# Rounding the weights in two stages: the first piece in two halves, and the first unit's scores ahead of the last sums

## The chip, the cores and the metric

The kernel runs on one core of one Trainium2 chip. The time of a run is the device time of that core in microseconds (us), and the metric is the median of several runs. A core has a matrix engine (PE, TensorE), three engines for element-wise work (DVE or VectorE, ACT or ScalarE, POOL or GpSimd), a queue that starts transfers (SP, SyncE) and 16 engines that carry them out. Each engine works through its own list of instructions in order and waits for the others by semaphores.

## The reference

Attention that keeps the 32 largest scores of every row, followed by a two-layer network with a leaky ReLU. There are 8 batches of 8 heads, with 576 positions and 64 values per head; the network has 4608 tokens, 512 inputs and 2048 hidden values.

```python
scores = scale * np.matmul(q, k.transpose(0, 1, 3, 2))
kth = np.partition(scores, -top_k, axis=-1)[..., -top_k:-top_k + 1]
scores = np.where(scores >= kth, scores, -1000000000.0)
attn = np.exp(scores - np.max(scores, axis=-1, keepdims=True))
attn = attn / (np.sum(attn, axis=-1, keepdims=True) + 1e-09)
x = np.matmul(attn, v)        # heads side by side: (4608, 512)
h = x @ w_in                  # (4608, 2048)
out = np.maximum(0.01 * h, h) @ w_out
```

The inputs q, k and v are 32-bit floats. The two weight matrices are 64-bit floats, and have to be turned into 32-bit floats by the kernel.

## The kernel before

**Rounding the weights (lines 84 to 150 and 492 to 511).** Both weight matrices together are cut into 16 pieces of 128 partitions by 1024 columns. Each 64-bit number is loaded as four 16-bit words, so a piece is 1 MB. `load_weights(n)` starts the load of piece n into one of three `raw` buffers. `round_weights(n)` is a generator with three stages:

- Stage 1: POOL copies the top word of each number into a 16-bit tile `top` (L124). ACT turns the third word into a float (L125), and the lower two words into a bf16 (L127).
- Stage 2: DVE takes the exponent out of `top` (L129, into the tile `scale`), the top bits of the mantissa (L132, into a tile that has the name `wT`), and the sign (L133, in place). ACT raises 2 to the exponent (L131). PE adds up the three parts of the mantissa: for each half of 512 columns three products with scaled identity matrices (L143, L144, L145), which the text calls the sums.
- Stage 3: DVE joins sign and power of two (L147) and multiplies the sums by it (L150).

The loop of lines 495 to 500 issues, in iteration n, stage 1 of piece n, stage 2 of piece n-1 and stage 3 of piece n-2. The order in which these calls are made is the order of the instructions on each engine. Then follows the load of piece n+3. The tiles `top` and `scale` have two buffers each, so POOL's copy for piece n waits until L147 of piece n-2 has read `top`. A load of piece n+3 waits until L124, L125 and L127 of piece n have read the raw buffer. PSUM holds the sums in the tiles `wide` (two buffers, pieces 0 to 11), `narrow` (one, pieces 12 and 14) and `ml` (two, pieces 13 and 15).

**The first scores.** In the iterations n = 12 to 15 the loads of q and k for the first four head pairs are started (`load_qk`), and the loads of v in n = 15. In iteration 14 `first_scores` issues the products of unit 0 (L231) on PE and the two copies of its scores from PSUM on ACT (L236); in iteration 16 it does so for unit 1.

**The rest.** A unit is 128 rows of queries of two heads. The main loop runs one step per unit: DVE finds the 32 largest scores (`top_k`, lines 238 to 255, which begins with L245), POOL masks, ACT takes exponents, the weights are transposed by transfers through DRAM, PE weighs the values, and PE works off the network for finished tokens in between, by budgets in the code. The order is written out by hand, nothing is reordered.

Of the kernel before, what the change touches and what calls it, by code (L numbers as in the profile page):

```python
# [20 lines left out]
def kernel(  # L21
# [78 lines left out]
    def load_weights(n):  # L100
        if n >= NPIECE:
            return
        if not AS_WORDS:
            nc.sync.dma_start(piece(n), weights[n])
            return
        raw_of[n] = raws.tile([P, WCH, 4], U16, name="raw")
        nc.sync.dma_start(raw_of[n].rearrange("p n w -> p (n w)"), weights[n])

    def round_weights(n):

        raw = raw_of.pop(n)
        dst = piece(n)
        mid = raw[:, :, 2]
        low = raw.rearrange("p n w -> p (n w)").bitcast(U32).rearrange("p (n w) -> p n w", w=2)[:, :, 0]
        top = raws.tile([P, WCH], U16, name="top", bufs=2)
        scale = raws.tile([P, WCH], U16, name="scale", bufs=2)  # L120
        parts = work.tile([P, 2 * NKC - 1, P], F32, name="wT", bufs=3)
        parts = parts.rearrange("p c n -> p (c n)").bitcast(U16)
        m_top, m_low = parts[:, 0:WCH], parts[:, WCH:2 * WCH].bitcast(BF16)
        nc.gpsimd.tensor_copy(top, raw[:, :, 3])  # L124
        nc.scalar.activation(dst, mid, AF.Copy, bias=-7.0 - 2.0 ** -16, scale=2.0 ** -20)  # L125

        nc.scalar.activation(m_low, low, AF.Copy, bias=128.0, scale=2.0 ** -29)  # L127
        yield
        nc.vector.tensor_scalar(scale, top, 4, 0x7FF, ALU.logical_shift_right, ALU.bitwise_and)  # L129

        nc.scalar.activation(scale.bitcast(BF16), scale, AF.Exp, bias=least, scale=LN2)  # L131
        nc.vector.tensor_scalar(m_top, top, 0xF, 0x3F80, ALU.bitwise_and, ALU.bitwise_or)  # L132
        nc.vector.tensor_scalar(top, top, 0x8000, None, ALU.bitwise_and)  # L133
        if n < NPIECE - 4 or n % 2 == 0:
            tag, bufs = ("wide", 2) if n < NPIECE - 4 else ("narrow", 1)
            pw = ps_sc.tile([P, 2, 512], F32, name=tag, bufs=bufs)
            sums = [(pw[:, h, :], h * 512) for h in range(2)]
            ends = [(pw.rearrange("p h n -> p (h n)"), 0)]
        else:
            ends = sums = [(ps_ml.tile([P, 512], F32, name="pw", tag="ml"), h * 512) for h in range(2)]  # L140
        for pw, c in sums:
            at = slice(c, c + 512)
            nc.tensor.matmul(pw, ident_top, m_top[:, at].bitcast(BF16), start=True, stop=False)  # L143
            nc.tensor.matmul(pw, ident, dst[:, at], start=False, stop=False)  # L144
            nc.tensor.matmul(pw, ident_low, m_low[:, at], start=False, stop=True)  # L145
        yield
        nc.vector.tensor_tensor(scale, scale, top, ALU.bitwise_or)  # L147
        for pw, c in ends:
            at = slice(c, c + pw.shape[-1])
            nc.vector.tensor_tensor(dst[:, at], pw, scale[:, at].bitcast(BF16), ALU.mult)  # L150
# [73 lines left out]
    def first_scores(u):  # L224

        ps = [ps_sc.tile([P, 2, 512], F32, name="wide", bufs=2) for i in range(2)]
        for half in range(2):
            for i, pi, side, r0 in u.parts:
                qt, kt = qk_of[pi]
                d = slice(side * D, (side + 1) * D)  # L230
                nc.tensor.matmul(ps[i][:, half, 0:HS], qt[d, u.q0:u.q0 + P],  # L231
                                 kt[d, half * HS:(half + 1) * HS], start=True, stop=True)
        u.both = work.tile([P, 2, S], F32, name="s_sb", bufs=5)
        u.s = [u.both[:, i, :] for i in range(2)]
        for i in range(2):
            nc.scalar.copy(u.s[i].rearrange("p (h n) -> p h n", h=2), ps[i][:, :, 0:HS])  # L236
# [243 lines left out]
    with tc.manual_schedule():  # L480
        last = {p: n for n, u in enumerate(steps) for p in u.pairs}

        def load_more(s):

            for of, load, n, lag in ((v_of, load_v, LOADED_V, LAG + 1), (qk_of, load_qk, LOADED + 3, 8)):
                while len(of) < NPAIR and (len(of) < n or last[len(of) - n] + lag <= s):
                    load(len(of))
                    if lag > LAG + 1 and len(of) > n:
                        break


        for n in range(3):
            load_weights(n)
        rounding = {}
        for n in range(NPIECE + 2):
            for i in (n, n - 1, n - 2) if AS_WORDS else ():
                if 0 <= i < NPIECE:
                    if i == n:
                        rounding[i] = round_weights(i)
                    next(rounding[i], None)  # L500
            load_weights(n + 3)

            if NPIECE - HP <= n < NPIECE:
                load_qk(n - NPIECE + HP)
            if n == NPIECE - 2:
                first_scores(steps[0])
            elif n == NPIECE:
                first_scores(steps[1])
            if n == NPIECE - 1:
                load_v(0)  # L510
                load_v(1)

        def weights_of(u):
            reciprocals(u)
            normalize(u, 0)
            normalize(u, 1)

        def values(*place):
            due = [u for n, u in enumerate(steps) if values_at(n) == place]
            if due:  # L520
                po = ps_sc.tile([P, 2, 512], F32, name="wide", bufs=2)[:, 0, 0:2 * P]
# [126 lines left out]
```

## Time and profile before

| | |
|---|---|
| median of 3 runs | 1468.14 us (1467.84 to 1468.83) |
| span of the profiled execution, first to last instruction | 1467.8 us |
| mean granted TensorE clock | 0.982 |
| busy, whole span | PE 1393.7 us (95%), DVE 1319.9 (90%), ACT 1099.8 (75%), POOL 1096.2 (75%) |
| busy, 0 to 63.54 us | PE 49.74 us, DVE 48.82, ACT 54.08, POOL 18.76; transfer engines 93% |
| moved by transfers | 222.29 MB, mean 151 GB/s; 342 GB/s from 0 to 63.54 us |

The span is the profiled execution's own time as the page gives it; the runs' median stands 0.3 us above it. At 63.54 us the first instruction of `top_k` starts on DVE, and the rounding of the weights is over. In the lines shown below, "L150 DVE ..." is line 150 of the kernel and the engine that runs it; an entry such as `w_in<-wide,scale` names the tile that is written and those that are read; "x2" says that a row joins two instructions; and a bracket gives how long the engine had been idle before, and the engine, tile and line that released it. The rows of digits cut the span in 40 slices and give the busy share of each in tenths.

### The profile page before, as it was taken

Reading aid. Unit: us, or ns where it says so; the run is one execution under the profiler, and the core shown is the slowest. Engines: PE = TensorE matmul, PEld = TensorE weight load, DVE = VectorE, ACT = ScalarE, POOL = GpSimd, SP = SyncE. Lnnn points to the kernel's source line nnn. Section 1 sums busy time; section 2 is a strip of 40 time slices with the busy share of each in tenths; the row PEclk is TensorE's granted clock in tenths of the full one; section 3 lists DMA queues with packets and bytes.
Section 4 is the critical chain, followed back from the end, with each engine's and each line's share of the span. In section 5 each row is a group of like instructions: output and inputs, shape, how many; then the busy total and the mean of one; then the engine's idle time right before and its main releaser. Section 6 shows DMA issues by size and latency. Waiting matters only on the chain.

```text
span 1467.8 us, 24094 instructions
## 1 busy us (share of the span) xinstructions
PE 1393.7 (95%) x8068; PEld 927.3 (63%) x8068; DVE 1319.9 (90%) x3396; ACT 1099.8 (75%) x1981; POOL 1096.2 (75%) x743
## 2 busy tenths in 40 slices
PE   7716999999999999999999999999999999999999
PEld 2304548575757676767676767666666666666674
DVE  6999999999999999999999999999999999999600
ACT  8657888777887777777777777777777777777710
POOL 3288888888788888787878888878787878787700
PEclk9957999999999999999999999999999999999999
DMA  9824443654376455664566544766566545664510
GB/s 332 299 81 130 138 119 112 174 153 137 101 194 192 129 137 155 171 185 137 146 170 190 141 137 129 191 178 150 127 168 200 140 135 138 161 138 136 146 46 14
DMA packets 388795, 222.29 MB, mean 151 GB/s; under 512 B 333888, under 2 KB 333888, under 8 KB 386624
## 3 DMA queue, kind: packets, MB, share of 16 engines
q1 hardware_dynamic: 388672, 220.77, 53.9%
q8 instruction: 63, 1.03, 0.3%
q14 instruction: 60, 0.49, 0.1%
HBM read 46.14 MB, written 92.01 MB: 94 GB/s over the span
## 4 chain that ended last, share of the span: by engine, by line
PE 85%; DVE 10%; ACT 2%; DMA 2%; issue 1%; POOL 0%; DVEq 0%; SPq 0%; ACTq 0%
PE ph L386 32%; PE pz L398 31%; PE wide L330 11%; PE wide L215 6%; DVE tops L250 3%; PE narrow L215 3%; DVE pairs L253 3%; DMA wT<-apart 1%; PE ph L354 1%; DVE pairs L245 1%; DVE w_in L150 1%; ACT split L288 1%; DVE scale L147 1%; ACT s_sb L222 1%; DVE w_out L150 1%
## 5 line engine op out<-in xcount | busy, mean ns | idle before, releaser
L263 POOL TENSOR_SCALAR pen<-s_sb,tops 128x576 f32<-128x576 f32 x288 | 637.5, 2214 | 209.2 <-DVE tops L250 139.0
L250 DVE MAX8 tops<-pairs 128x8 f32<-128x288 f32 (+1 forms) x1152 | 635.9, 591 | 0.0
L398 PE MATMUL pz<-w_out,gT 128*128 128x512 f32 x1152 | 504.7, 594 | 2.4 <-ACT scale L359 2.4
L386 PE MATMUL ph<-x,w_in 128*128 128x256 f32 x2176 | 482.7, 381 | 0.0
L253 DVE MATCH_REPLACE8 pairs<-tops,pairs 128x288 f32<-128x288 f32 (+1 forms) x864 | 460.1, 538 | 0.0
L386 PEld LDWEIGHTS ph<-x,w_in 128*128 128x128 f32 x2176 | 409.4, 190 | 76.5 <-issue 22.2
L264 POOL TENSOR_TENSOR s_sb<-s_sb,pen 128x576 f32<-128x576 f32 x288 | 406.5, 1412 | 24.1
L398 PEld LDWEIGHTS pz<-w_out,gT 128*128 128x128 f32 x1152 | 216.4, 190 | 267.2 <-issue 262.8
L288 ACT COPY split<-s_sb 128x1152 uint16<-128x1152 uint16 x280 | 309.4, 1146 | 0.0
L279 ACT ACTIVATE s_sb<-s_sb,rz 128x576 f32<-128x576 f32 x288 | 207.6, 772 | 45.5 <-DVE rz L276 45.5
L267 ACT ACTIVATE s_sb<-s_sb,nbias 128x576 f32<-128x576 f32 x288 | 222.2, 772 | 15.2 <-POOL s_sb L264 15.2
L245 DVE TENSOR_TENSOR pairs<-s_sb 128x576 f32<-128x576 f32 x288 | 213.4, 780 | 10.3 <-ACT s_sb L279 0.5
L330 PEld LDWEIGHTS wide<-wT,vt 128*64 128x64 f32 x3200 | 161.2, 139 | 68.0 <-issue 35.0
L330 PE MATMUL wide<-wT,vt 128*64 128x128 f32 (+1 forms) x3200 | 179.0, 268 | 25.5 <-ACT s_sb L222 22.1
L222 ACT COPY s_sb<-wide 128x704 f32<-128x704 f32 x142 | 107.1, 755 | 21.4 <-PE wide L215 21.4
L392 ACT ACTIVATE gT<-ph 128x512 f32<-128x512 f32 x136 | 80.6, 592 | 54.2 <-PE ph L386 53.5
L344 ACT COPY x<-wide 128x128 f32<-128x128 f32 (+1 forms) x160 | 32.2, 260 | 112.9 <-PE wide L330 112.8
L215 PE MATMUL wide<-kt,qt 64*128 64x352 f32 (+1 forms) x392 | 74.6, 490 | 28.8 <-ACT s_sb L222 24.9
L407 ACT COPY o_sb<-pz 128x512 f32<-128x512 f32 x36 | 21.1, 585 | 97.5 <-PE pz L398 97.5
L222 ACT COPY s_sb<-narrow 128x448 f32<-128x448 f32 x142 | 68.7, 536 | 0.7
L276 DVE RECIPROCAL rz<-ze 128x2 f32<-128x2 f32 x144 | 22.2, 154 | 45.7 <-ACT ze L272 45.5
L253 DVE MATCH_VALUE_LOAD pairs<-tops,pairs 128x8 f32 x864 | 62.5, 72 | 0.0
(61 smaller groups left out, 623.2 us busy)
## 6 DMA issues: line engine op xcount, KB each, us to landing
apart<-split SPq DMA_DIRECT2D x280, 288.0 KB, 2.1
raw<-in_weights_dram SPq DMA_DIRECT2D x16, 1024.0 KB, 5.8
vt<-in_vk_dram SPq DMA_DIRECT2D x32, 320.0 KB, 3.8
out_dram<-o_sb SPq DMA_DIRECT2D x36, 256.0 KB, 2.6
qt<-in_qT_dram SPq DMA_DIRECT2D x20, 288.0 KB, 3.5
kt<-in_kT_dram SPq DMA_DIRECT2D x20, 288.0 KB, 3.7
raw<-in_qT_dram SPq DMA_DIRECT2D x12, 288.0 KB, 3.5
raw<-in_kT_dram SPq DMA_DIRECT2D x12, 288.0 KB, 3.8
```

What stands on the lines that cost most here:

```text
L215: nc.tensor.matmul(to[r0:r0 + u.rows, i, :], qt[d, u.q0:u.q0 + u.rows], kt[d, k0:k1], start=True, stop=True)
L245: nc.vector.tensor_tensor(pairs[:, :, n, :], u.both[:, :, 0:HS], u.both[:, :, HS:S], op)
L250: nc.vector.max(out=u.tops[:, i, r, :], in_=rest[i])
L253: nc.vector.match_replace(out=rest[i], in_to_replace=u.tops[:, i, r, :], in_values=rest[i], imm_value=LOWEST)
L263: nc.gpsimd.tensor_scalar(pen, u.s[i], u.tops[:, i, ROUNDS - 1, 7:8], MASKED, ALU.is_lt, ALU.mult)
L264: nc.gpsimd.tensor_tensor(u.s[i], u.s[i], pen, ALU.add)
L267: nc.scalar.activation(u.s[i], u.s[i], AF.Exp, bias=u.nbias[:, i:i + 1], scale=SCALE, accum_out=u.z[:, i:i + 1])
L279: nc.scalar.activation(u.s[i], u.s[i], AF.Copy, bias=0.0, scale=u.rz[:, i:i + 1])
L288: nc.scalar.copy(split, pairs[:, :, h])
L330: nc.tensor.matmul(po[side * D:(side + 1) * D, o, :], vt[:, c, side, :], u.wT[:, c + side * NKC if c + 1 < NKC else c, r:r + n], start=(c ...
L386: nc.tensor.matmul(ph[:, i, 0:n], w_in[c][:, f * P:(f + 1) * P], x[c][:, 0:n], start=(c == 0), stop=(c == HP - 1),)
L398: nc.tensor.matmul(pz[0:m, 0:DMODEL], gT[:, f, r0:r0 + m], w_out[f // 4][:, f % 4, :], start=(f == 0), stop=(f == NFC - 1),)
```

## The change

The generator has two stages instead of three. The first one now holds all that was in stages 1 and 2: POOL's copy, DVE's three operations, ACT's two conversions and its exponent, and PE's sums. The second is what was stage 3. ACT's exponent of a piece thus stands behind its own two conversions, and no longer behind those of the next piece.

The work is cut into 17 jobs: piece 0 is two jobs of 512 columns, each with its own load; the other 15 pieces are one job each. Job n's first stage is issued with job n-1's second stage behind it.

`first_scores` is a generator as well. The products of unit 0 are issued in the last job's iteration, in front of that job's first stage, and its copies after it; unit 1 follows in the iteration behind. The loads of q and k for the first pairs are issued behind the weight loads of the same iteration: pair 0 between the loads of pieces 14 and 15, pairs 1 to 3 behind the load of piece 15.

```diff
+        flat = raw_of[n].rearrange("p n w -> p (n w)")
+        for m, c0, c1 in ROUNDED:
+            if m == n:
+                nc.sync.dma_start(flat[:, 4 * c0:4 * c1], weights[n][:, 4 * c0:4 * c1])
+
+    ROUNDED = [(0, 0, WCH // 2), (0, WCH // 2, WCH)] + [(n, 0, WCH) for n in range(1, NPIECE)]
+
+    def round_weights(n, c0, c1):
...
         nc.gpsimd.tensor_copy(top, raw[:, :, 3])
-        nc.scalar.activation(dst, mid, AF.Copy, bias=-7.0 - 2.0 ** -16, scale=2.0 ** -20)
-
-        nc.scalar.activation(m_low, low, AF.Copy, bias=128.0, scale=2.0 ** -29)
-        yield
         nc.vector.tensor_scalar(scale, top, 4, 0x7FF, ALU.logical_shift_right, ALU.bitwise_and)
-
-        nc.scalar.activation(scale.bitcast(BF16), scale, AF.Exp, bias=least, scale=LN2)
         nc.vector.tensor_scalar(m_top, top, 0xF, 0x3F80, ALU.bitwise_and, ALU.bitwise_or)
         nc.vector.tensor_scalar(top, top, 0x8000, None, ALU.bitwise_and)
+        nc.scalar.activation(dst, mid, AF.Copy, bias=-7.0 - 2.0 ** -16, scale=2.0 ** -20)
+
+        nc.scalar.activation(m_low, low, AF.Copy, bias=128.0, scale=2.0 ** -29)
+
+        nc.scalar.activation(scale.bitcast(BF16), scale, AF.Exp, bias=least, scale=LN2)
...
                 nc.tensor.matmul(ps[i][:, half, 0:HS], qt[d, u.q0:u.q0 + P],
                                  kt[d, half * HS:(half + 1) * HS], start=True, stop=True)
+        yield
         u.both = work.tile([P, 2, S], F32, name="s_sb", bufs=5)
...
+        jobs = [round_weights(*job) for job in ROUNDED] if AS_WORDS else [iter(())] * len(ROUNDED)
+        for n in range(len(jobs) + 1):
+            if n == len(jobs) - 1:
+                first = first_scores(steps[0])
+                next(first, None)
+            for job in jobs[max(n - 1, 0):n + 1][::-1]:
+                next(job, None)
+            if n == len(jobs) - 1:
+                next(first, None)
                 load_v(0)
                 load_v(1)
+            elif n == len(jobs):
+                for _ in first_scores(steps[1]):
+                    pass
+            if n:
+                load_weights(n + 2)
+            if 0 <= n - len(jobs) + HP + 1 < HP:
+                load_qk(n - len(jobs) + HP + 1)
```

In the changed kernel the lines behind the edit have moved: DVE's first three operations are L131, L132 and L133, its last two L152 and L155, ACT's L134, L136 and L138, POOL's copy L130, the sums L148 to L150, and `top_k` begins with L251.

More of the change, by code (lines that the diff above doesn't have):

```diff
@@ L106, in load_weights @@
         raw_of[n] = raws.tile([P, WCH, 4], U16, name="raw")
[L107 to L116, printed above, removed]
+        flat = raw_of[n].rearrange("p n w -> p (n w)")
[4 more added lines that the diff above has]
+    def round_weights(n, c0, c1):
+        raw = raw_of[n][:, c0:c1, :]
+        dst = piece(n)[:, c0:c1]
+        wide = c1 - c0
         mid = raw[:, :, 2]
-        low = raw.rearrange("p n w -> p (n w)").bitcast(U32).rearrange("p (n w) -> p n w", w=2)[:, :, 0]
-        top = raws.tile([P, WCH], U16, name="top", bufs=2)
-        scale = raws.tile([P, WCH], U16, name="scale", bufs=2)
+        low = raw_of[n].rearrange("p n w -> p (n w)").bitcast(U32).rearrange("p (n w) -> p n w", w=2)[:, c0:c1, 0]
+        top = raws.tile([P, WCH], U16, name="top", bufs=2)[:, 0:wide]
+        scale = raws.tile([P, WCH], U16, name="scale", bufs=2)[:, 0:wide]
         parts = work.tile([P, 2 * NKC - 1, P], F32, name="wT", bufs=3)
         parts = parts.rearrange("p c n -> p (c n)").bitcast(U16)
-        m_top, m_low = parts[:, 0:WCH], parts[:, WCH:2 * WCH].bitcast(BF16)
+        m_top, m_low = parts[:, 0:wide], parts[:, WCH:WCH + wide].bitcast(BF16)
         nc.gpsimd.tensor_copy(top, raw[:, :, 3])
+        nc.vector.tensor_scalar(scale, top, 4, 0x7FF, ALU.logical_shift_right, ALU.bitwise_and)
+        nc.vector.tensor_scalar(m_top, top, 0xF, 0x3F80, ALU.bitwise_and, ALU.bitwise_or)
+        nc.vector.tensor_scalar(top, top, 0x8000, None, ALU.bitwise_and)
         nc.scalar.activation(dst, mid, AF.Copy, bias=-7.0 - 2.0 ** -16, scale=2.0 ** -20)
         nc.scalar.activation(m_low, low, AF.Copy, bias=128.0, scale=2.0 ** -29)
-        yield
-        nc.vector.tensor_scalar(scale, top, 4, 0x7FF, ALU.logical_shift_right, ALU.bitwise_and)
         nc.scalar.activation(scale.bitcast(BF16), scale, AF.Exp, bias=least, scale=LN2)
-        nc.vector.tensor_scalar(m_top, top, 0xF, 0x3F80, ALU.bitwise_and, ALU.bitwise_or)
-        nc.vector.tensor_scalar(top, top, 0x8000, None, ALU.bitwise_and)
         if n < NPIECE - 4 or n % 2 == 0:
@@ L136, in round_weights @@
             pw = ps_sc.tile([P, 2, 512], F32, name=tag, bufs=bufs)
-            sums = [(pw[:, h, :], h * 512) for h in range(2)]
-            ends = [(pw.rearrange("p h n -> p (h n)"), 0)]
+            sums = [(pw[:, c // 512, :], c) for c in range(0, wide, 512)]
+            ends = [(pw.rearrange("p h n -> p (h n)")[:, 0:wide], 0)]
         else:
@@ L493 @@
             load_weights(n)
[L494 to L509, printed above, removed]
+        jobs = [round_weights(*job) for job in ROUNDED] if AS_WORDS else [iter(())] * len(ROUNDED)
[7 more added lines that the diff above has]
+                next(first, None)
                 load_v(0)
                 load_v(1)
+            elif n == len(jobs):
[5 more added lines that the diff above has]
+                load_qk(n - len(jobs) + HP + 1)
         def weights_of(u):
```

## The prediction

> **What bounds the kernel now.** I read the page's chain of waits first, then the long chain in order of time, then the timeline of each engine over the first 66 us, and last the waits of PE and DVE in the rest.
>
> ```profile
> PE   7716999999999999999999999999999999999999
> DVE  6999999999999999999999999999999999999600
> ...
> PE 85%; DVE 10%; ACT 2%; DMA 2%; issue 1%; POOL 0%; DVEq 0%; SPq 0%; ACTq 0%
> ```
>
> The whole run is PE work at the end and DVE work at the start. The waits of DVE from 63 to 250 us, and of PE from 250 us to the end, tell how stiffly the start is tied to the end:
>
> ```profile
> DVE rz L276 <- ACT ze L272: 0.2, 1, 0.2
> ...
> PE wide L330 <- DMA wT<-apart: 2.4, 3, 0.9
> ```
>
> From 63 us DVE waits 0.2 us in 187 us, and from 250 us PE waits 2.4 us in 1218 us. So when the first `top_k` starts on DVE, everything behind it follows at a fixed distance; a microsecond off the rounding of weights is a microsecond off the run. That start is 63.54 us here. In the rounding the DVE lines are these (start, length, and in brackets the idle time before it with its releaser):
>
> ```profile
> 9.26 0.43 DVE L129 TENSOR_SCALAR scale<-top 128x1024 uint16<-128x1024 uint16 x1 [1.25 <-POOL top L124]
> ...
> 11.31 0.69 DVE L147 TENSOR_TENSOR scale<-scale,top 128x1024 uint16<-128x1024 uint16 x1 [0.83 <-ACT scale L131]
> 12.92 1.22 DVE L150 TENSOR_TENSOR w_in<-wide,scale 128x1024 f32<-128x1024 f32 x1 [0.91 <-PE wide L145]
> 14.25 0.43 DVE L129 TENSOR_SCALAR scale<-top 128x1024 uint16<-128x1024 uint16 x1
> ...
> 17.51 0.43 DVE L129 TENSOR_SCALAR scale<-top 128x1024 uint16<-128x1024 uint16 x1
> ...
> 57.09 0.43 DVE L129 TENSOR_SCALAR scale<-top 128x1024 uint16<-128x1024 uint16 x1
> ...
> 59.61 0.69 DVE L147 TENSOR_TENSOR scale<-scale,top 128x1024 uint16<-128x1024 uint16 x1 [1.29 <-ACT scale L131]
> ...
> 63.54 1.42 DVE L245 TENSOR_TENSOR pairs<-s_sb 128x576 f32<-128x576 f32 x2
> ```
>
> Call T(n) the start of L129 for piece n. T(1) = 9.26, T(2) = 14.25, T(3) = 17.51, T(5) = 24.02, T(15) = 57.09. From T(2) on the step is 3.26 us, DVE being full: 0.34 + 0.45 + 0.34 + 0.79 + 1.34 between the starts of its five instructions. Idle time stands only at the two ends: between T(1) and T(2), 4.99 us instead of 3.26, and before the last-but-one L147. The second has its cause on ACT and PE:
>
> ```profile
> 54.07 1.22 PE wide L231 x8
> 55.29 1.16 ACT s_sb L236 x2
> 56.45 1.05 ACT w_out L125
> 57.50 1.04 ACT wT L127
> 58.54 1.04 ACT scale L131
> ```
>
> Unit 0's copies (L236) stand in ACT's queue in front of the last piece's L125 and L127 and of the exponent for piece 14 (L131), and wait for score products that PE has behind piece 13's sums.
>
> **What the Trainium skill says.** "TensorE: Matmul & The Clock Gate", Part 1, says that PE runs at half clock until a free-running window of about 3.4 us has been busy, and, under the architectural detail, that ACT and DVE are strict first-in first-out. The trace agrees: a pair of L144 products takes 1.92 us from 7.98 us and 1.02 us from 14.59 us, the switch being near 13.3 us, 5.7 us after PE's first product; and ACT's copies block an exponent whose input is there. "VectorE: DVE Perf Modes", What auto-detection actually checks, gives one-source 16-bit operations two modes where two-source ones have one, so the lengths of a half piece fall by different amounts; the trace has 0.43 (L129), 0.68 (L147) and 1.23 us (L150) for 1024 columns, and 0.69 us for L150 with 512. "DMA: Bandwidth & Descriptors", Rules for kernel authors, says that two transfers to the two partition halves of a tile serialize on the same 16 engines. The change splits columns, not partitions, and no split transfer is in this trace; I take the halves to arrive one after the other.
>
> **The change part by part.**
>
> (a) The first stage in one go. For piece n, POOL's copy, the three DVE operations, ACT's three and PE's sums are now issued together, and the last two DVE operations one piece later. DVE's order in the steady state is the same as before (three operations of n, then two of n-1), so the 3.26 us step stays. What is late next? POOL's copy needs the `top` buffer of n-2, that is L147 of n-2, and lies beside the 1.23 us of L150 as it does now (1.13 us). ACT has 3 x 1.04 = 3.12 us per piece, below 3.26, though the exponent of n now waits on ACT for DVE's first operation of n, with the next piece's two conversions queued behind it; it may start at T(n)+0.5, ends at T(n)+1.6 and is wanted at T(n)+4.4. PE starts at T(n)+0.8, takes 2.6 and is wanted at T(n)+5.2. So the steady state costs nothing; its thinnest cover is ACT's 0.14 us per piece.
>
> (b) The first piece in halves. A 1 MB piece lands every 2.5 us at first (5.60, 8.07, 10.5). Half 0 should land at 5.60 - 1.25 = 4.35, half 1 at 5.6, piece 1 at 8.07 as now. Half lengths: POOL and ACT 0.6, DVE 0.29 and 0.42 (from the slopes above), L150 0.69, sums 2.5 at the cold clock. Half 0: copy to 5.0, DVE to 5.9, PE 5.65 to 8.2. Half 1: copy to 6.25, exponent to 7.6, PE 8.2 to 10.7. Piece 1: copy 8.1 to 9.2, T(1) = 9.3, as now. Then half 1's L147 stands at 9.3 + 1.13 = 10.4 instead of piece 0's at 11.31: its exponent is long done. It ends at 10.85; POOL copies piece 2 from 10.9 to 12.0, T(2) = 12.1. Half 1's L150 (11.0 to 11.7) fits in front. From there T(3) = 15.4 against 17.51, 2.1 us gained. PE can spoil it: piece 1's sums run from 10.7, and its L150 is wanted at 14.1. With the clock warm 3.4 to 6.8 us after 5.65, they end at 13.3 to 14.3, a loss of 0 to 0.25.
>
> (c) The loads. A raw buffer comes free with ACT's L127, now at T(n)+0.45 instead of T(n)-0.2, so each later load goes out 0.65 us later in its piece's cycle. It is wanted by POOL at T(n+3)-1.4, which leaves 7.8 us; issue to landing was 4.7 to 7.5 us from the fourth piece on. Piece 5 is the tight one: issued at 13.37, and again at 13.4 after the change, since piece 2 is converted at the same time in both; it landed 7.5 us later:
>
> ```profile
> 20.91 1.17 ACT L125 ACTIVATE w_in<-raw 128x1024 f32<-128x1024 uint16 x1 [0.28 <-DMA raw<-in_weights_dram]
> ```
>
> T(5) would be 12.1 + 9.8 = 21.9 and needs the copy at 20.5; with landing at 20.87 it becomes 20.9 + 1.13 + 0.1 = 22.15. So 1.87 us of the 2.1 are left (24.02 - 22.15). I take that; the ends are 1.3 (another 0.5 lost to later landings) and 2.15 (piece 5 lands sooner). The loads of q and k for pair 0 now go in front of weight piece 15 on SP. They move 0.6 MB, 1.5 us at the first pieces' rate; piece 15 lands near 52 and is wanted near 53.5, so that is hidden; if not, it costs its lateness on DVE.
>
> (d) Unit 0's scores in front of the last sums. PE ends the sums of piece 14 at T(15)+0.16, multiplies the scores (eight products, 1.22 us) to T(15)+1.4 and then starts piece 15's sums, 0.6 later than their inputs allow. ACT's copies of the scores come after the last exponent, which ends at T(15)+1.6. The sums of piece 15 end at T(15)+4.0, and the second L150 of that piece is wanted at T(15)+4.5: covered by 0.5. So DVE runs on: from T(15), 1.14 to L147 of 14, then 0.79 + 1.14 + 0.79 + 1.21 to `top_k`, 5.07 us, where it now takes 63.54 - 57.09 = 6.45. Gain 1.38, which is the stall's 1.29 and its hand-over. Unit 1's scores are ready 1.7 us after `top_k` 0 starts, and wanted 8.8 us after.
>
> Sum: 1.87 + 1.38 = 3.25 us. The span is 1467.8 and the median of the runs 1468.14, 0.3 above; 3.25 off the median is 1464.9.
>
> **The rivals.**
>
> Rival 1, a part of the gain is lost at the start: cold PE, later landings or a slower first half. For it: a transfer's landing varied by 2.8 us, and landings from piece 2 to piece 7 were 3.36 us apart (16.8/5), more than DVE's step. Against: landings then catch up (the time from issue falls to 4.7 us), so supply is not the limit afterwards. At 3.36 through piece 15: 10.5 + 13 x 3.36 = 54.2, T(15) = 55.6, gain 1.5 + 1.38 = 2.9, and less with any cold PE: 1465.3 to 1467, centre 1466.0. This is no change, as 0.2% (2.9 us) is what a measurement here can tell.
>
> Rival 2, slower: the weights' supply becomes the bound, because each raw buffer is released 0.65 us later. A load has 7.8 us; each three pieces lose what it takes above that, four times over. At 8.6 us this eats the 3.25, from there it is slower; at 9.3 us it costs 4 x 1.5 = 6.0, giving 1470.9. For it: the third load took 8.9 us. Against: that one was queued behind two others at once, and the median is 5.8.
>
> Rival 3, the merge does not remove the stalls because ACT, blocked in order by its exponents, becomes the bound: a step of 3.4 over 13 pieces would lose 1.8, leaving 1466.7. Against: 3.12 of 3.26.
>
> **How the numbers follow.** Forecast 0.62 (1463.9 to 1465.2), rivals 1 and 3 together 0.28, rival 2 and its like 0.10. The forecast lies only 0.3 us beyond the 0.2% bound, so faster 0.62, same 0.28, slower 0.10. Below 1463.7 nearly nothing is left (all of 2.15 + 1.38 gives 1464.6, a sooner landing and the runs' scatter of 1 us the rest); up to 1467.3 takes in rivals 1 and 3.
>
> **What would show it.** `T(2)`, now L131 on DVE, near 12.1 and `T(5)` near 22.1; DVE idle in front of L152 for the last pieces gone; the first L251 at 60.3; ACT waiting on weights at piece 5; and the rest of the chain unchanged. The prediction is wrong if DVE's step rises above 3.26, or if L251 starts at 60.3 and the span does not follow.

## The result, and the profile after

The changed kernel has a median of 1467.63 us over 20 runs (1466.55 to 1469.5). The kernel before, run beside it, has 1470.1 us over 20 runs (1467.48 to 1473.9). The ratio is 0.9984, with a 95% interval of 0.9977 to 0.999: a gain of 2.5 us by the medians. The forecast was 1464.9 us and the range ended at 1467.3, so the time lies 0.3 us outside. Most of the 2.73 us between forecast and result is not the change: 1470.1 - 1468.14 = 1.96 us is the kernel before, whose first three runs were low ones of its own spread, and 0.78 us is a gain of 2.47 where 3.25 was forecast.

The page of the changed kernel, with the same three rows as before (busy tenths of PE and DVE in 40 slices, and the shares of the chain that ended last):

```profile
PE   7617999999999999999999999999999999999999
DVE  7999999999999999999999999999999999999600
...
PE 81%; DVE 16%; ACT 1%; issue 1%; DMA 0%; POOL 0%; DVEq 0%; SPq 0%; ACTq 0%; POOLq 0%
```

The kernel is bound as it was, by DVE at the start and by PE at the end; the share of DMA on the chain has gone from 2% to 0%. DVE's timeline of the changed kernel answers to the one in the prediction (start, length, operation, and the idle time before it with its releaser):

```profile
10.23 0.43 DVE L131 TENSOR_SCALAR scale<-top 128x1024 uint16<-128x1024 uint16 x1 [0.70 <-POOL top L130]
...
13.03 0.43 DVE L131 TENSOR_SCALAR scale<-top 128x1024 uint16<-128x1024 uint16 x1 [0.44 <-POOL top L130]
...
16.29 0.43 DVE L131 TENSOR_SCALAR scale<-top 128x1024 uint16<-128x1024 uint16 x1
...
55.87 0.43 DVE L131 TENSOR_SCALAR scale<-top 128x1024 uint16<-128x1024 uint16 x1
...
57.01 0.68 DVE L152 TENSOR_TENSOR scale<-scale,top 128x1024 uint16<-128x1024 uint16 x1
...
60.94 1.42 DVE L251 TENSOR_TENSOR pairs<-s_sb 128x576 f32<-128x576 f32 x2
```

These are T(1), T(2), T(3), T(15), the last L152 but one, and the first `top_k`. T(1) was 9.26 and is 10.23: the first full piece is *later* than before, by 0.97 us. Both stalls that the change aimed at are gone: T(1) to T(2) takes 2.80 us instead of 4.99, and L152 has no bracket where L147 had waited 1.29. `top_k` starts at 60.94 instead of 63.54, 2.60 us earlier: 1.22 from the start (57.09 - 55.87), 1.38 from the end.

Why T(1) is late can be seen on ACT and in the chain in order of time. ACT's first conversion of the first half and of piece 1:

```profile
4.83 0.66 ACT L134 ACTIVATE w_in<-raw 128x512 f32<-128x512 uint16 x1 [2.84 <-DMA raw<-in_weights_dram]
...
8.95 1.15 ACT L134 ACTIVATE w_in<-raw 128x1024 f32<-128x1024 uint16 x1 [0.56 <-DMA raw<-in_weights_dram]
```

The changed kernel's chain up to 20 us, of which this is the transfer it hangs on (start, length, what):

```profile
1.64 7.29 DMA raw<-in_weights_dram
```

Piece 1's load was issued third, at 1.64 us, and landed at 8.93; in the kernel before ACT started on piece 1 at 8.09. The whole early chain of the changed kernel hangs on this one landing, and no longer on DVE and PE. The transfers of the first 12 us, in slices of 0.3 us, show a part of the reason; first the kernel before, then the changed one (GB/s moved):

```profile
GB/s 0 0 0 0 0 164 218 0 109 355 437 437 437 437 410 410 410 437 437 382 410 437 410 437 437 410 437 437 437 410 410 437 437 219 218 328 437 437 437 437
```

```profile
GB/s 0 0 0 0 0 27 96 164 328 314 232 191 259 341 423 423 396 382 423 369 437 382 437 437 382 410 437 437 437 410 437 437 437 437 437 355 382 382 437 437
```

Before, the rate is 437 from the eleventh slice (3.0 us) and not below 382 from there to 9.9 us. After, it is 191 to 341 in the ninth to fourteenth slice, 2.4 to 4.2 us, and reaches 423 only from 4.2 us. Added up, the changed kernel is 0.19 MB behind at 4.2 us and 0.23 MB at 8.1 us; at 437 GB/s that is, by estimate, 0.5 us of the 0.86 by which ACT starts later on piece 1. Piece 1 was also issued later, at 1.64 instead of 1.2 us. A half of the piece has rows of 4 KB where a whole piece has 8 KB. The Trainium skill bears on both sides of this, in "Perfetto Trace Analysis", DMA Optimizations: splitting a transfer may let work start sooner, with a gain for the whole if the transfer engines are otherwise idle, and larger transfers use the memory better. Here two more loads are queued behind the first, and both sides are in the numbers: the first half is there 0.8 us sooner (4.83 against 5.62), and the next piece 0.86 later (8.95 against 8.09).

### The profile page after: what moved, and what is told of

It reads as the page before. It is cut to its first block, busy times and chain, and to the rows that moved or that the text cites. A ratio compares the mean times of both kernels' runs of the same rounds, so it can differ in the third digit from the quotient of the medians.

```text
span 1465.2 us, 24106 instructions
## 1 busy us (share of the span) xinstructions
PE 1395.2 (95%) x8066; PEld 927.8 (63%) x8068; DVE 1320.3 (90%) x3401; ACT 1100.4 (75%) x1984; POOL 1097.0 (75%) x744
## 4 chain that ended last, share of the span: by engine, by line
PE 81%; DVE 16%; ACT 1%; issue 1%; DMA 0%; POOL 0%; DVEq 0%; SPq 0%; ACTq 0%; POOLq 0%
PE pz L404 31%; PE ph L392 30%; PE wide L336 10%; DVE tops L256 6%; PE wide L220 6%; DVE pairs L259 5%; PE narrow L220 3%; DVE pairs L251 2%; DVE w_out L155 1%; DVE scale L152 1%; DVE w_in L155 1%; DMA raw<-in_weights_dram 0%; DVE top L133 0%; DVE scale L131 0%; ACT s_sb L285 0%
## 5 line engine op out<-in xcount | busy, mean ns | idle before, releaser
L251 DVE TENSOR_TENSOR pairs<-s_sb 128x576 f32<-128x576 f32 x288 | 213.5, 780 | 9.9
```

Source lines behind the costliest of these rows:

```text
L251: nc.vector.tensor_tensor(pairs[:, :, n, :], u.both[:, :, 0:HS], u.both[:, :, HS:S], op)
```

## The experiments

**The load whole, the rounding still in halves.**

```diff
-        for m, c0, c1 in ROUNDED:
-            if m == n:
-                nc.sync.dma_start(flat[:, 4 * c0:4 * c1], weights[n][:, 4 * c0:4 * c1])
+        nc.sync.dma_start(flat, weights[n])
```

> The changed kernel, but piece 0 comes in one transfer of 1 MB again; it is still rounded in two halves. Theory A (splitting the first load made every early load later): piece 1 lands at 8.1 us instead of 8.95, the first DVE operation of piece 1 starts at 9.3 instead of 10.23, that of piece 2 at 12.1 to 12.5 instead of 13.03, and the first operation of top_k at 60.0 to 60.4 instead of 60.94; the span falls by 0.5 to 0.9. Rival B (the late landing was this one execution's, or comes of the other order of instructions): piece 1 lands at 8.9 again and top_k starts at 60.9 or later, since the first half now also waits for the whole piece.

Measured: 1467.78 us (21 runs) against 1469.34 (25), ratio 0.9988 (0.9981 to 0.9995); `top_k` at 61.45 us. The landing came back as expected (6.9 us after the issue at 1.2, so at 8.1), and POOL copied piece 1 at 8.64 us, as soon as DVE gave its `top` buffer free. But T(1) did not follow. DVE's timeline of this kernel:

```profile
6.28 0.70 DVE L129 TENSOR_SCALAR scale<-top 128x512 uint16<-128x512 uint16 x1 [4.60 <-POOL top L128]
...
9.99 0.69 DVE L153 TENSOR_TENSOR w_in<-wide,scale 128x512 f32<-128x512 f32 x1 [1.41 <-PE wide L148]
10.79 0.43 DVE L129 TENSOR_SCALAR scale<-top 128x1024 uint16<-128x1024 uint16 x1
```

and PE's for the first sums:

```profile
7.62 1.91 PE L147 MATMUL wide<-w_in,ident 128*128 128x512 f32 x2
```

T(1) is 10.79, without idle time of its own: it is queued behind L153 of the first half, which waits 1.41 us for sums that PE does at half clock (1.91 us for a pair that takes 1.02 later). With the whole load PE starts at 7.24 instead of 6.09, so its slow time falls where DVE needs it; 0.41 us of this is DVE's first operation, 0.70 us long instead of 0.29 (see the last section). The split load had hidden this: what it cost in landing it paid back in an earlier start of PE. So the expectation was wrong in all that follows the landing: T(1) is 10.79 and not 9.3, T(2) 13.57 and not 12.1 to 12.5, `top_k` 61.45 and not 60.0 to 60.4.

**No halves at all, two stages.** Sixteen jobs, piece 0 in one.

```diff
-    ROUNDED = [(0, 0, WCH // 2), (0, WCH // 2, WCH)] + [(n, 0, WCH) for n in range(1, NPIECE)]
+    ROUNDED = [(n, 0, WCH) for n in range(NPIECE)]
...
-            if n:
-                load_weights(n + 2)
+            load_weights(n + 3)
```

> The changed kernel without halves: 16 jobs, piece 0 loaded and rounded whole. Theory: with two stages alone nothing is gained at the start, because PE at half clock still needs 5.1 us for piece 0's sums from 7.8 us on, so that the last product of piece 0 waits until 12.9 us and piece 2 begins on DVE at 14.2 us, as in the kernel before; top_k starts at 62.2 (63.54 less the 1.38 of the end). Rival (the gain at the start was the exponent's place in ACT's queue, not the halves): piece 2 begins at 12.5 or sooner and top_k starts at 60.4.

Measured in one execution: T(1) = 9.15, T(2) = 13.64, `top_k` at 61.53, time 1469.09. T(1) is early, as a whole first load makes it; then L155 of piece 0 waits 1.34 us for PE, until 12.31, and T(2) is queued behind it. The mechanism is the theory's, but T(2) and `top_k` came 0.6 and 0.7 us sooner than it said, since PE came up to full speed within its second pair of products (1.69 us instead of 1.91). In this pair of executions the halves are worth 0.6 us of T(2) net (13.64 against 13.03).

**Only the load split, in the kernel before.** Two column halves for piece 0, everything else as before.

```diff
-        nc.sync.dma_start(raw_of[n].rearrange("p n w -> p (n w)"), weights[n])
+        flat = raw_of[n].rearrange("p n w -> p (n w)")
+        if n == 0:
+            nc.sync.dma_start(flat[:, 0:2 * WCH], weights[n][:, 0:2 * WCH])
+            nc.sync.dma_start(flat[:, 2 * WCH:4 * WCH], weights[n][:, 2 * WCH:4 * WCH])
+        else:
+            nc.sync.dma_start(flat, weights[n])
```

> The kernel before, with the load of piece 0 alone cut into two transfers by columns (rows of 4 KB instead of 8 KB); nothing else is changed, piece 0 is still rounded whole. Theory A (the two transfers of 4 KB rows make every early load later): ACT's first conversion starts at 6.3 instead of 5.62 and that of piece 1 at 8.9 instead of 8.09, top_k 0.7 to 0.9 later than 63.54. Rival B (the late landings in the changed kernel had another cause): both start within 0.2 us of the kernel before.

Measured in one execution: T(1) = 10.12 instead of 9.26, 0.86 later, with nothing else of the change present; `top_k` at 64.38, 0.84 later; time 1471.52, span 1469.5. The halves landed 4.0 and 5.1 us after their issue and piece 1 7.3 us after its own at 1.64. The split load alone makes the delay of T(1). A second thing shows on ACT's timeline:

```profile
6.36 1.28 ACT L130 ACT_TABLE_LOAD   x1 [6.36 <-DMA raw<-in_weights_dram]
```

The table load stood at 0.72 us in the kernel before; here, where the first conversion has two transfers to wait for, it waits for them too, and ACT converts only from 7.66 (so T(2) and `top_k` are not the split's doing alone; the expected 6.3 for the first conversion was missed by this). In the next kernel it stands at 9.61.

**The same split by partitions.** Two transfers of 64 partitions with rows of 8 KB; the edit is shown against the column split.

```diff
-            nc.sync.dma_start(flat[:, 0:2 * WCH], weights[n][:, 0:2 * WCH])
-            nc.sync.dma_start(flat[:, 2 * WCH:4 * WCH], weights[n][:, 2 * WCH:4 * WCH])
+            nc.sync.dma_start(flat[0:P // 2], weights[n][0:P // 2])
+            nc.sync.dma_start(flat[P // 2:P], weights[n][P // 2:P])
```

> The kernel before, with the load of piece 0 cut into two transfers by partitions (64 rows of 8 KB each). Theory A1 (it is the length of the rows, 4 KB, that costs): piece 1's first conversion starts within 0.2 us of 8.09. Theory A2 (it is the number of transfers, one more issue on SP and one more completion in front): it starts at 8.5 to 8.9, as with the columns.

Both expectations failed: the second half landed 8.2 us after its issue, T(0) is 10.78 and T(1) 13.02; time 1473.62. The transfers of its first 12 us:

```profile
GB/s 0 0 0 0 0 0 82 328 410 273 300 137 218 137 191 191 355 55 273 55 246 137 273 246 300 137 246 191 273 300 410 437 382 410 437 437 382 382 437 437
```

The rate stays between 55 and 355 from the tenth slice to the thirtieth, 216 on average, half of a whole piece's 437. Rows of 8 KB are no help if a transfer covers 64 partitions, so this run doesn't separate row length from the number of transfers; the next one takes the number alone.

**One more transfer, with no split.** The kernel before with a transfer of 16 KB, read by nothing, between the loads of pieces 0 and 1.

```diff
+        extra = small.tile([P, 64], U16, name="extra", bufs=1)
         for n in range(3):
             load_weights(n)
+            if n == 0:
+                nc.sync.dma_start(extra, weights[NPIECE - 1][:, 0:64])
```

> The kernel before with one more small transfer (128 rows of 128 bytes, 16 KB, into a tile that nothing reads) issued between the loads of pieces 0 and 1. Theory A1 (short rows, not one more transfer, made the early loads late): piece 0 lands as before, and POOL's copy of piece 1 starts within 0.3 us of 8.11. Theory A2 (one more transfer in front, with its issue of 0.45 us on SP): the copy of piece 1 starts at 8.5 to 9.0.

Measured in one execution: POOL's copy of piece 1 at 8.29 us instead of 8.11, T(1) = 9.45 instead of 9.26; time 1471.44. One more issue and one more small transfer cost 0.2 us, so the other 0.7 of the 0.9 comes of how the 1 MB itself is moved as two halves. That it is the length of the rows, and not that each transfer is half as large, no run shows.

**PE warm, no halves.** Sixteen jobs as above, and 13 products of the identity with itself on PE from 1.34 us, whose result nothing reads. PE is called warm when a pair of products takes its short time, 1.02 us, and cold when it takes 1.9.

```diff
+    WARM = 13
...
+        idle = ps_ml.tile([P, 512], F32, name="pw", tag="ml")
+        for _ in range(WARM):
+            nc.tensor.matmul(idle[:, 0:P], ident, ident, start=True, stop=True)
```

> One piece, two stages (piece 0 whole), with 13 products of the identity with itself on PE from 1.6 us on, into a PSUM tile that nothing reads. Theory (in the run without halves the start is bound by PE's half clock): the clock is full by 8.4 us, piece 0's last product starts at 11.2 instead of 12.31, piece 2 begins on DVE at 12.5 instead of 13.64 (changed kernel: 13.03), and top_k at 60.4 to 60.6 (changed kernel: 60.94), if no load is late. Rival (loads, not PE, are next): piece 2 begins at 12.5 but piece 4 or 5 waits for its load and top_k starts at 61 or later.

DVE's timeline of this kernel:

```profile
9.42 0.43 DVE L132 TENSOR_SCALAR scale<-top 128x1024 uint16<-128x1024 uint16 x1 [1.22 <-POOL top L131]
...
12.69 0.43 DVE L132 TENSOR_SCALAR scale<-top 128x1024 uint16<-128x1024 uint16 x1
```

T(2) - T(1) is 3.27, the full step: PE no longer holds up L156 of piece 0. T(15) = 55.53 and `top_k` 60.59, 0.35 earlier than in the changed kernel, without halves. Time 1467.82 (13 runs), ratio 0.999 (0.9981 to 0.9998). The first pair of sums takes 1.02 us here. So the halves were a cure for PE's slow start, and a warm PE makes them needless up to `top_k`; by the times the two kernels are not told apart.

**The changed kernel once more, unaltered.**

> The changed kernel once more, unaltered, to see what of its start repeats: piece 1's first conversion at 8.95 within 0.15 us, the first operation of piece 2 at 13.0, top_k at 60.9 if no load is late and up to 0.7 later where one is; the time 2.4 us below the kernel before, within 1.

Measured: 1467.67 us (21 runs) against 1469.88 (33), ratio 0.9982 (0.9976 to 0.9989). Its profile has two waits that the first one hadn't: 0.39 us at T(4) and 0.42 at T(15), both for POOL's copy and with it for a late load, and `top_k` at 61.40 instead of 60.94. So late loads cost 0 in one execution and 0.8 in another. That the later release of the raw buffers makes them late is not shown: loads are late in the kernel with three stages too (there DVE's L147 waited 0.74 and 0.28 us for ACT, whose conversions had waited for loads, in one execution with the scores moved).

**Unit 0's scores one piece earlier.** Products in front of piece 14's sums, copies before the last conversions.

```diff
-            if n == len(jobs) - 1:
+            if n == len(jobs) - 2:
                 first = first_scores(steps[0])
...
-            if n == len(jobs) - 1:
+            if n == len(jobs) - 2:
                 next(first, None)
+            if n == len(jobs) - 1:
                 load_v(0)
```

> The changed kernel with unit 0's scores one job earlier: products in front of piece 14's sums, copies behind piece 14's exponent, so that ACT meets them before the last piece's conversions, as in the kernel before. Theory A (the end was shortened because a piece's exponent no longer stands behind the next piece's conversions; the place of the scores matters little): top_k starts within 0.3 us of the changed kernel's 60.94. Rival B (the place of the scores alone made the gain): the stall of 1.3 us in front of the last pieces' sign-and-exponent operation returns and top_k starts at 62.2.

Measured in one execution: from T(15) to `top_k` 5.06 us, as in the changed kernel (5.07). With the stages merged, the place of the scores no longer matters. `top_k` itself is at 61.58, outside the 0.3 us that were expected, since loads were late here too: 0.57 us at T(4) and 0.36 at T(7). Time 1467.24.

**Three stages, only the scores moved.** The products of unit 0 go in front of the last piece's sums and the copies behind, in the kernel before; first in one execution, then in 20.

```diff
+        yield
...
+            if n == NPIECE:
+                first = first_scores(steps[0])
+                next(first, None)
             for i in (n, n - 1, n - 2) if AS_WORDS else ():
...
-            if n == NPIECE - 2:
-                first_scores(steps[0])
-            elif n == NPIECE:
-                first_scores(steps[1])
+            if n == NPIECE:
+                next(first, None)
+                for _ in first_scores(steps[1]):
+                    pass
```

> The kernel before, three stages and piece 0 whole, with only unit 0's scores moved: products in front of the last piece's sums, copies behind the last exponent. Theory: the stall of 1.29 us before the last-but-one sign-and-exponent operation goes and top_k starts at 62.2 instead of 63.54, the rounding up to the last piece unchanged (its first DVE operation at 57.1). Rival (the stall needs the two stages to go): top_k starts at 63.5.

> Three stages as before, only unit 0's score products moved in front of the last piece's sums. Its one execution so far started top_k 1.47 us earlier (62.07 against 63.54) and yet had a span of 1468.7 against 1467.8. Theory 'passes through': what comes behind top_k follows at a fixed distance but for a scatter of about a microsecond from execution to execution that has nothing to do with the change; then the median over five rounds lies 1.2 to 1.7 us under that of the kernel before, ratio 0.9988 to 0.9992. Rival 'the end is set elsewhere': the rest of the kernel doesn't follow the first top_k; then the median is within 0.4 us of before, ratio 0.9997 to 1.0003, and what the whole change gained came from something other than the earlier start. T(15) about 57.0 and top_k about 62.1 in its profile in both.

One execution: `top_k` at 62.07, 1.47 us earlier than before, but a time of 1470.84. Of 20 runs the median is 1467.76 us (1465.44 to 1470.61) against 1469.4 (24), ratio 0.9988 (0.9981 to 0.9995). In the profile of these, T(15) is 57.67 and `top_k` 62.73, 0.6 us later than expected because of the late loads just named; from the one to the other it takes 5.06 us. The stall is gone here as well, on DVE's timeline of the second of these:

```profile
58.80 0.68 DVE L147 TENSOR_TENSOR scale<-scale,top 128x1024 uint16<-128x1024 uint16 x1
...
62.73 1.42 DVE L246 TENSOR_TENSOR pairs<-s_sb 128x576 f32<-128x576 f32 x2
```

So either edit alone removes the stall at the end, the moved scores here and the merged stages in the run above, where the scores stand near their old place; the change does it twice. And the gain passes through in the median (1.64 us), though a single execution can hide it. This small edit is not told apart from the whole change: each against the kernel before that ran beside it, it gained 1.64 us and the whole change 2.47 and 2.21, and the intervals of the ratios overlap (0.9981 to 0.9995; 0.9977 to 0.999 and 0.9976 to 0.9989).

**Where the start's gain goes afterwards.** This was read from the traces. DVE has one reciprocal per unit, 144 in all; its start, less that in the kernel before, follows the gain through the run (us):

| unit (its time before) | changed | changed, again | scores moved, first execution | PE warm, no halves |
|---|---|---|---|---|
| 0 (86) | -2.59 | -2.14 | -1.46 | -2.94 |
| 24 (297) | -2.58 | -2.12 | -1.40 | -3.07 |
| 25 (307) | -1.39 | -0.93 | -0.21 | -3.05 |
| 48 (516) | -1.40 | -0.94 | 1.07 | -3.05 |
| 107 (1061) | -1.56 | -0.69 | 1.41 | -2.15 |
| 108 (1072) | -2.68 | -1.80 | 0.99 | -2.98 |
| 143 (1390) | -2.79 | -1.91 | 0.90 | -3.01 |

At 297 us the gain is within 0.13 us of what it was at 86. Then 1.19 us are lost in one step in three of the columns, and not in the fourth. PE shows why, some 110 us earlier. Its timeline for the first products of one unit's scores and what goes before them, in the kernel before and in the changed one:

```profile
195.17 1.98 PE L398 MATMUL pz<-w_out,gT 128*128 128x512 f32 x4 [2.14 <-ACT scale L359]
197.08 0.82 PE L215 MATMUL wide<-kt,qt 64*64 64x352 f32 x8
```

```profile
192.31 2.42 PE L404 MATMUL pz<-w_out,gT 128*128 128x512 f32 x4 [2.14 <-ACT scale L365]
194.66 1.45 PE L220 MATMUL wide<-kt,qt 64*64 64x352 f32 x8
```

The same eight products take 0.82 and 1.45 us. The windows of the changed kernel (stretch, length, then busy time and instructions of PE, its weight loads, DVE, ACT and POOL, the granted clock of PE, the share of DMA, GB/s):

```profile
190.00:192.00 2.00, 0.17 (x2) 0.00 (x0) 2.00 (x6) 2.00 (x5) 1.83 (x3) 1.00 0.94 212
192.00:194.00 2.00, 1.69 (x4) 0.68 (x4) 1.97 (x4) 2.00 (x3) 0.96 (x2) 0.93 0.04 8
194.00:196.00 2.00, 2.00 (x13) 0.65 (x16) 2.00 (x6) 1.81 (x5) 1.92 (x2) 0.50 0.59 222
196.00:198.00 2.00, 2.00 (x29) 1.02 (x21) 2.00 (x9) 1.24 (x3) 1.90 (x2) 0.72 0.19 73
```

PE is idle for 2.14 us from 190.17, and after that its clock is halved for 0.07 x 2 / 0.5 + 2 + 0.28 x 2 / 0.5 = 3.4 us. The kernel before has the same gap of 2.14 us (from 193.03) and a clock of 1.00 throughout. What PE loses here stays lost: it has hardly a wait left from 250 us on, and DVE, which runs ahead of it, meets the loss at unit 25. The step at unit 108 is the kernel before's own: there PE had waited 0.89 us for a transfer into `wT`, and the changed kernel didn't. From 250 us to the end PE's waits in the changed kernel (us in total, times, longest) are only this, where the kernel before had 2.4 us for `wT`:

```profile
PE ph L392 <- ACT gT L398: 0.9, 1, 0.9
```

The loss of 1.28 between units 25 and 48 in the third column, not in the others, comes with 2.5 us of waits of PE for `wT` between 430 and 520 us; with the 1.19 it is why that one execution had no gain at its end. The smaller steps were not followed one by one. "TensorE: Matmul & The Clock Gate", Part 1, What's actually happening, has such a window of about 3.4 us, free-running, after which an idle PE falls to half clock. The length agrees. That a whole window must be idle does not agree with a gap of 2.14 us, and here the measurement decides.

Of the 14 profiled executions of all kernels 8 have the half clock between 192 and 200 us and 6 haven't: the kernel before, the two with sixteen jobs, the one with the earlier scores, the split by partitions, and the last one below. The link to unit 25 holds in all of them: from unit 24's reciprocal to unit 25's it takes 10.97 to 11.18 us in those 8, and 9.70 to 10.01 in the 6. All 14 have the gap of 2.13 or 2.14 us. What decides was not settled. That it is the position of PE's gap against that window is argued, not shown.

**The best of it together.** The load whole, halves, 12 identity products on PE at the start, and the loads of q and k one iteration later, behind all weights.

```diff
...
-            if 0 <= n - len(jobs) + HP + 1 < HP:
-                load_qk(n - len(jobs) + HP + 1)
+            if 0 <= n - len(jobs) + HP < HP:
+                load_qk(n - len(jobs) + HP)
```

> The changed kernel with piece 0 in one transfer of 8 KB rows, still rounded in two halves, with 12 products of the identity on PE from 1.4 us on (read by nothing), and with the first loads of q and k one iteration later, so that pair 0's follow weight piece 15. Theory: with the clock full and rows of 8 KB the start comes where the prediction had it: piece 1 begins on DVE at 9.4 to 9.6, piece 2 at 12.2 to 12.5, top_k at 60.0 to 60.4 if no load is late; the median 0.4 to 1.0 us below the changed kernel's. Rival (the loads are the next bound): a load is late for pieces 4 to 7 and top_k starts at 60.8 or later.

Measured: 1467.28 us (21 runs) against 1469.39 (41), ratio 0.9985 (0.9978 to 0.9991). PE's first sums and DVE's T(1) in this kernel:

```profile
7.47 1.02 PE L148 MATMUL wide<-w_in,ident 128*128 128x512 f32 x2
```

```profile
9.83 0.43 DVE L130 TENSOR_SCALAR scale<-top 128x1024 uint16<-128x1024 uint16 x1 [0.39 <-POOL top L129]
```

The pair takes 1.02 us from the first, no load is late, and `top_k` starts at 60.51, 3.03 us before that of the kernel before. T(1), T(2) (12.61) and `top_k` are each 0.1 to 0.2 us later than the theory's latest. The gain in time, 2.1 us, is not larger than the changed kernel's. Its trace has the half clock from 192.8 us.

**PE warm at another place.** The same with 18 identity products at 116 us, in front of the values of units 2 and 3 (at 124 us), where PE's clock was also low.

```diff
+            if place == (7, MIDDLE):
+                idle = ps_ml.tile([P, 512], F32, name="pw", tag="ml")
+                for _ in range(18):
+                    nc.tensor.matmul(idle[:, 0:P], ident, ident, start=True, stop=True)
```

> The same, with 18 more products of the identity on PE in front of the values of units 2 and 3 (step 7), where PE is idle for 8 us at half clock. Theory (PE's clock at 124 to 131 us is what moves the time behind the start from run to run, by up to 2 us): the 40 products of the values take 2.4 to 3 us instead of 3.7 to 4.5, and the median falls by a further 0.5 to 1.5 with a smaller spread. Rival (DVE is the chain there, PE has slack): the 40 products are shorter and the median is the same within 0.5.

Measured: 1467.13 us (21 runs), ratio 0.9985 (0.9978 to 0.9991). The 40 products there take 2.40 us instead of 4.21, and nothing measurable comes of it (1467.13 against 1467.28), as the rival had it: PE has slack at this place. This is the lowest median, but neither of these two kernels can be told from the changed one.

## Why the prediction was wrong, step by step

Two terms were mis-sized: in (b) the landing of the halves, and the base from which the gain was taken. The base is the larger part of the miss. That the two stalls would go, and how, was right.

**What bounds the kernel.** Right about the start; the sentence that everything behind follows at a fixed distance was too strong. It rested on DVE's waits from 63 to 250 us and PE's from 250 us. Neither view shows PE before 250 us, nor its clock. The profiled pair agrees by accident: 2.60 us at the start and 1467.8 - 1465.2 = 2.6 in the span, but in between 1.19 us were lost at 194 us and about as much was won where the kernel before had waited for transfers. In the medians of the timed executions the span falls by 1.6 to 1.9 us.

**(a) The two stages.** Right. The step stayed 3.26 us (13.03 to 16.29), and ACT's 0.14 us per piece was cover enough.

**(b) The halves.** This is the step of the gain that failed: "half 0 should land at 5.60 - 1.25 = 4.35, half 1 at 5.6, piece 1 at 8.07 as now". The first half landed at 4.83, the second at 6.3, and piece 1 at 8.93. The rate of whole pieces had been carried over to transfers of half the size with rows half as long. What follows from the landing was right: T(2) - T(1) was forecast as 2.8 and is 2.80, T(3) came one step later, and PE's cold clock cost nothing on top. But all three are 0.9 late. The split of the load alone in the kernel before shows the same 0.86.

What the halves were to gain was measured against one execution, and T(2) = 14.25 is the latest of four. In the three others that round piece 0 whole in three stages with a whole load (one small transfer more; scores moved, twice) T(2) is 13.63, 14.20 and 13.63. In the last of them, with the scores moved, PE came to full speed sooner, and L150 does not wait for it:

```profile
10.48 1.02 PE L144 MATMUL wide<-w_in,ident 128*128 128x512 f32 x2
```

In the profile that the prediction read, this pair begins at 10.54 and takes 1.92 us. So 0.6 of the 2.1 us hung on when PE's clock came up in that execution. It did not last there: T(15) is 57.06, 57.01 and 57.67, against 57.09, with late loads in the two whose T(2) was early. With the halves T(2) is 13.03, 12.91 and 12.99 in three executions, though the second pair of products takes 1.21, 1.02 and 1.91 us in them. Nor is 3.4 us after PE's first product the earliest, as the prediction had it: with the load whole PE begins at 7.24 and is at full speed by 10.04, 2.8 us later.

**(c) The loads.** Piece 5, the tight one of the forecast, was not late: T(5) = 22.81 is T(3) + 2 x 3.26, since DVE came 0.9 later as well. So of the gain at the start 24.02 - 22.81 = 1.21 is left where 1.87 was taken; the 0.66 are the 0.91 of the landing less the 0.25 that had been charged to piece 5. That no load was late was luck in part: in two later executions one was, at T(4), by 0.39 and 0.57 us. That piece 15's load, behind q and k, "costs its lateness" if it isn't hidden came true in the second profile, with 0.42 us.

**(d) The scores.** Right to the hundredth: 5.07 us from T(15) to `top_k`. That each of the two edits does this alone was not seen.

**The base.** "The span is 1467.8 and the median of the runs 1468.14, 0.3 above" took three runs for the kernel's time. In every later set of runs of the kernel before the time lies 2.0 us above the span of the same execution (medians of the sets, 2.00 to 2.05), so an execution with this span takes about 1469.8; the later medians are 1469.34 to 1470.1. This is the other step that failed, 1.96 of the 2.73 us, and a range worked out from such a base is 1 to 2 us too low whatever the change does. The band given to the forecast, 1463.9 to 1465.2, does not hold its own worst case either: 1.3 + 1.38 = 2.68 us off 1468.14 is 1465.5.

**The rivals.** The first, a part lost at the start through later landings, is what happened: it had the gain at 2.9 us, measured 2.60, though through the split and not through the spacing of landings it named. Loads as the bound and ACT as the bound didn't come.

## What to carry to other kernels

A load that is split so that work can start sooner has to be priced by when the *next* transfer lands, at the rate that the halves reach; splitting only the computation, with PE kept warm, avoided that price up to `top_k` (60.51 against 60.94), though not measurably in time. Where two edits remove the same stall, try the smaller alone: here moving eight products and two copies gained 1.64 us where the whole change gained 2.2 to 2.5, with about 1 us of uncertainty. And take the time before from as many runs as its spread asks for, since three runs lay 2 us under the median of twenty, nearly as much as the change was worth.

## What the hardware showed that was not expected

- With the first piece in two loads of 128 rows of 4 KB, 191 to 341 GB/s were moved from 2.4 to 4.2 us, where a whole piece with rows of 8 KB had 437 from 3.0 us; with it in two transfers of 64 partitions, 55 to 355 (216 on average) from 2.7 to 9.0 us.
- DVE's first operation on half a piece took 0.70 us instead of 0.29 where POOL's second copy ran beside it (5.62 to 6.84 us; the operation ended at 6.98). "SBUF — State Buffer", SBUF: two separate sides, says that POOL and, in some modes, DVE share a pair of ports as an exclusive lock, held for the whole instruction; an operation that ends just after the copy agrees with it, and the last two kernels above have the same (0.69 and 0.70 us).
- PE's clock fell to half between 192 and 198 us after a gap of 2.14 us in 8 of 14 traces, for 3.4 us in the changed kernel.
- PE was at full speed 2.8 us after its first product in the kernel with the load whole, and not yet 5.5 us after it in the kernel before (the pair at 13.10 us still took 1.22). The column of the granted clock reads 1.00 in the kernel before for all of the first 63.54 us, and so doesn't show this slow start: only the lengths do (1.92 us for a pair, then 1.02).
- DVE stalls once by 0.52 to 0.53 us with nothing to wait for: at T(8), 33.00 us, after the change and at T(9), 37.48, before. Both are the 46th row of DVE's timeline, and it is the 46th row in all 14 traces. No cause is known.
- The time outside the span is 2.0 us before and 1.77 to 1.82 in the kernels with 17 jobs (medians), while those with 16 have 1.97 to 2.09. So 0.2 us of the gain in time isn't in any trace.
